# First batch's odd value tiles copied on GpSimd, block sums stored by one DMA each, and all instruction lists replaced

## The chip, the cores and the metric

The kernel runs on one core of one Trainium2 chip. The metric is the device time of one execution in microseconds (us). Before the change three runs took 917.28, 917.82 and 918.20 us (median 917.82). The profile comes from one further execution of 918.29 us; the span of its trace, from the first to the last profiled instruction, is 916.5 us, so 1.79 us lie around it.

## The reference

Windowed causal attention over 8 batches, 8 heads, 576 positions and 64 channels, followed by an RMS norm and a gated feed-forward layer over all 4608 tokens (512 channels, 1536 hidden):

```python
scores = (1 / sqrt(64)) * q @ k.T                    # per batch and head, 576 x 576
mask = (rel >= 0) & (rel < 64)                       # each position sees itself and the 63 before it
attn = softmax(where(mask, scores, -1e9))
x = (attn @ v).transpose(0, 2, 1, 3).reshape(4608, 512)
xn = x / sqrt(mean(x * x, -1) + 1e-6) * rms_g
g, val = xn @ w_gate, xn @ w_val                     # 512 -> 1536
out = (g * sigmoid(g) * val) @ w_out                 # 1536 -> 512
```

## The kernel before, in words

**Attention.** Heads go in pairs, n = 4 * batch + pair, since two heads of 64 channels fill 128 partitions. Tiles `q`, `kv` come by DMA; `kv` holds the keys (576 columns), the "even" value blocks (640 columns) and the "odd" ones (512 columns), which are the same values shifted by half a block of 64 rows, so that a window of two neighbouring blocks can always be read as one tile of 128 partitions. In `load_kv`, `odd_values()` loads them from DRAM a second time, by two DMAs of 64 partitions for each pair. TensorE (PE) makes the scores (`sc`), VectorE (DVE) masks them and finds the row's extreme (the custom operation into `p` or `pm`), ScalarE (ACT) takes the exponential and its row sum into `st`, DVE inverts the sum, and a scaling follows: for batches 0 and 1 on GpSimd (POOL), from then on on ACT. The weights are turned by TensorE (`tr`, copied out to `pt`) in batches 0 and 1. From batch 2 on, 32 x 32 blocks are moved between partitions (`moved`: 13 or 16 copies for a pair, dealt to POOL and ACT by the string `MOVE_ON`) and then turned by DVE. Products with the values (`xp`) follow, are copied to `xb`, squared and summed (`ssq`), the total goes through TensorE (`tot`), a chain of small DVE steps makes the inverse root, `rb` spreads it, and `xn` holds the normalised tokens as two float16 parts.

**Feed-forward.** There are nine tiles of 512 tokens. The weights come as float32 by DMA (`st`), are widened, scaled and split in two float16 parts (`wt`). Tiles 0 and 1 are plain products: `pg` and `pv` (gate and value), `th` (gated result), `h`, `po` (output), each by three float16 products. From tile 2 (`FIRST7`) on, the input side takes 7 block products in place of 8 (`bk`), from tile 3 the output side too. These need sums of weight blocks. `prepare(c, step)` makes them for the six columns c of the input weights while tile 1 runs: DVE adds blocks into `sum0`, `sum1` and `blk`; its inner `out` lets ACT round a sum to float16 (`hl`, first half), DVE subtract for the second half, and SP store both halves by two DMAs to the DRAM tile `sevens`. Three of the seven blocks need no sum; they are copied there from `wt` by 12 DMAs for each column (72 in all). `load_sevens` loads the blocks into a ring of 15 places in `wt`, refilled as TensorE is done with them. `prepare_out` does the same for the output weights (`wsum`, `whl`, `outs`) while tile 2 runs.

**Order.** Each engine runs its instructions in the order in which they stand, SP its DMA issues too. All calls are first recorded under names (engine letter and tile, `t` TensorE, `v` DVE, `s` ACT, `g` POOL, `y` SP), and `emit_recorded` writes them out in the order of five literal lists, `ORDER` and `ORDER_0` to `ORDER_3`. The waits follow from the data and from the buffers: `t2k`, for instance, is a pool of 8 tiles of 2 KB per partition that `th`, `hl`, `blk`, `whl`, `ot`, `p` and others share, and a tile that a DMA stores is free once the DMA has landed. `keep_warm` records up to 24 times 40 idle products (`warm`, 256 columns of ones, read by nobody); the lists take as many of them as they name, 26 before. Every recorded instruction carries the line of the helper that emits it, 589 before and 591 after; tiles tell them apart.

Of the kernel before, what the change touches and what calls it, by code (L numbers as in the profile page):

```python
# [27 lines left out]
P = 128  # L28
# [3 lines left out]
NKT = 5  # L32
# [30 lines left out]
MOVE_ON = "ga"  # L63
# [32 lines left out]
g.blocked y.q_3 y.kv_0*3 y.kv_1 t.sc_0_0*7 y.st_0_0 t.sc_0_0 v.gmx v.shifted v.ebias t.sc_0_0 v.one t.sc_0_0 v.pick  # L96
t.sc_0_1 v.ebias v.shifted t.warm_0 v.p_0_0_0 t.warm_0 y.kv_1 t.warm_0 v.p_0_0_0 s.p_0_0_0 v.p_0_0_0 y.st_1_0 v.p_0_0_1
t.sc_0_1*2 v.p_0_0_1 s.p_0_0_0 t.sc_0_1*2 v.p_0_0_0 y.kv_3 t.sc_1_0 s.p_0_0_1 t.sc_0_1*3 y.kv_2 t.warm_0*2 v.p_0_1_1
s.p_0_0_1 t.warm_0 y.kv_2 v.p_0_1_1 v.p_0_1_0 s.p_0_0_0 t.sc_1_0 y.kv_2 t.sc_1_0 v.p_0_1_0 t.sc_1_0*5 s.p_0_1_1
t.sc_1_0 y.q_4 t.sc_1_0 v.st_0_0 t.gps v.st_0_0 v.first_of v.p_1_0_0 s.p_0_1_0 v.floor y.st_0_1 v.first_of g.p_0_0_1  # L100
v.p_1_0_0 v.gmx y.kv_3 s.p_0_1_0 v.p_1_0_0 g.p_0_0_0 v.p_1_0_0 t.tr_0_0_1*2 y.kv_3 s.p_0_1_1 t.sc_1_1*2 v.pt_0_0_1
t.sc_1_1*3 g.p_0_0_0 t.sc_1_1*2 s.p_1_0_0 t.sc_1_1 v.st_0_1 v.p_1_0_1 t.tr_0_0_0*2 v.st_0_1 s.p_1_0_0 v.p_1_0_1
t.tr_0_0_0 g.p_0_1_0 v.p_1_1_1 t.sc_2_0 v.p_1_1_1 s.p_1_0_0 v.pt_0_0_0 t.sc_2_0 g.p_0_1_1 s.p_1_0_1 v.pt_0_0_0
v.p_1_1_0 t.tr_0_1_0 v.p_1_1_0 s.p_1_0_1 t.tr_0_1_0 t.tr_0_1_1 v.gmx t.tr_0_1_1 t.sc_2_0 s.p_1_1_0 t.xp_0_0 t.sc_2_0*2
v.st_1_0 t.sc_2_0 v.unit t.sc_2_0*4 v.st_1_0 t.xp_0_0 v.unit s.p_1_1_1 t.xp_0_0*2 v.p_2_0_0 g.p_1_0_1 t.xp_0_0*3
v.p_2_0_0 t.xp_0_0 s.p_1_1_1 t.sc_2_1 v.p_2_0_0*2 g.p_1_0_0 v.pt_0_1_0 t.sc_2_1 v.first_of t.sc_2_1*2 s.p_1_1_0
t.sc_2_1*2 v.p_2_0_1 t.xp_0_0*2 t.sc_2_1 g.p_1_0_0 s.p_2_0_0 t.sc_2_1 v.pt_0_1_1 t.tr_1_0_0 v.p_2_0_1 t.xp_0_1
# [419 lines left out]
def tile_window_attention_moe(  # L527
# [456 lines left out]
    def weigh(part, low, total):  # L984
        nc.scalar.activation(part, part, AF.Exp, bias=low, scale=-1.0, accum_out=total)
# [1207 lines left out]
```

## Time and profile before

| | |
|---|---|
| median of three runs | 917.82 us |
| profiled execution / span of its trace | 918.29 us / 916.5 us |
| TensorE busy | 898.9 us (98%) |
| VectorE busy | 715.9 us (78%) |
| ScalarE busy | 672.3 us (73%) |
| GpSimd busy | 376.5 us (41%) |
| DMA, mean over the span | 212 GB/s |

"Busy" of PE covers the modelled ends of pipelined products, so a stretch with PE busy throughout may still hold fewer products than another. The columns of a window row are the stretch, its length, then busy time and number of instructions of PE, weight loads, DVE, ACT and POOL, the granted clock of TensorE as a share of full, the busy share of the 16 DMA engines, and GB/s.

### The profile page before, as it was taken

The page shows a single profiled execution, that of the slowest core. Times are in us where ns is not written, and L with a number is a line of the kernel's source. Part 1 is how long each engine was busy: PE and PEld are TensorE (multiplying, and loading weights), DVE is VectorE, ACT ScalarE, POOL GpSimd, SP SyncE. Part 2 cuts the span into 40 slices and gives each one's busy share as a digit, 9 for nine tenths or more (in the row PEclk, how much of TensorE's full clock was granted, in tenths as well). Part 3 has the DMA queues.
Part 4 walks back from the last instruction along what each step waited for, and adds up shares of the span by engine and source line. Part 5 has one row for each costly group of instructions (what it writes and reads, how often), then busy time and mean ns, then how long its engine had stood idle before and what let it go on. Part 6 is the DMA issues. An engine that isn't in the chain of part 4 may idle for free.

```text
span 916.5 us, 24146 instructions
## 1 busy us (share of the span) xinstructions
PE 898.9 (98%) x8861; PEld 688.2 (75%) x8872; DVE 715.9 (78%) x2026; ACT 672.3 (73%) x1777; POOL 376.5 (41%) x506
## 2 busy tenths in 40 slices
PE   7899999999999999999999999999999999999998
PEld 4655554444448884688888888888888888888887
DVE  5898879799988888689879877888788767724760
ACT  5888988497877798699869986998697435614550
POOL 3456445354353464155524543454345222311230
PEclk9999999999999999999999999999999999999999
DMA  9695666676326985497877886777766767777623
GB/s 298 212 281 169 236 201 159 188 216 207 116 82 203 316 276 156 133 370 235 278 226 229 234 280 220 233 233 248 225 186 188 238 193 202 202 242 207 176 72 112
DMA packets 130854, 194.26 MB, mean 212 GB/s; under 512 B 30896, under 2 KB 60592, under 8 KB 130736
## 3 DMA queue, kind: packets, MB, share of 16 engines
q1 hardware_dynamic: 130160, 191.84, 68.4%
q8 instruction: 69, 1.13, 0.5%
q10 hardware_dynamic: 576, 0.88, 0.3%
q14 instruction: 49, 0.40, 0.1%
HBM read 166.73 MB, written 25.95 MB: 210 GB/s over the span
## 4 chain that ended last, share of the span: by engine, by line
PE 86%; DVE 7%; ACT 4%; DMA 2%; issue 1%; SPq 0%; ACTq 0%; POOL 0%; DVEq 0%
PE bk L589 59%; PE pv L589 6%; PE pg L589 6%; PE xp L589 4%; PE sc L589 4%; PE po L589 3%; ACT pm L589 2%; DVE th L589 1%; DVE wt L589 1%; DVE pm L589 1%; PE tr L589 1%; PE pw L589 1%; DVE ssq L589 1%; DVE sum L589 1%; DMA q<-q 1%
## 5 line engine op out<-in xcount | busy, mean ns | idle before, releaser
L589 PEld LDWEIGHTS <-wt 128*128 128x128 f16 x4128 | 402.4, 98 | 112.8 <-issue 8.1
L589 PE MATMUL bk<-xn,wt 128*128 128x256 f16 x2016 | 242.5, 273 | 1.8 <-DVE th L589 1.7
L589 PE MATMUL bk<-wt,wt 128*128 128x256 f16 x1440 | 176.9, 273 | 0.0
L589 POOL TENSOR_TENSOR hw<-th,hw 128x256 f16<-128x256 f32 x72 | 66.0, 934 | 254.1 <-ACT hw L589 194.2
L589 PE MATMUL bk<-hw 128*128 128x256 f16 x1512 | 169.4, 273 | 0.6 <-ACT ot L589 0.6
L589 PEld LDWEIGHTS <-hw 128*128 128x128 f16 x1512 | 146.7, 98 | 18.7 <-issue 1.8
L589 ACT ACTIVATE pm<-pm,st 128x128 f32<-128x128 f32 (+1 forms) x432 | 151.4, 388 | 8.3 <-DVE st L589 7.8
L589 POOL COPY pm<-pm 32x288 f32<-32x288 f32 (+1 forms) x169 | 84.0, 497 | 77.1 <-ACT pm L589 70.7
L589 ACT ACTIVATE th<-bk,hsc 128x256 f32<-128x256 f32 x126 | 59.3, 472 | 33.2 <-DVE bk L589 17.5
L589 DVE SCALAR_TENSOR_TENSOR th<-th,bk 128x256 f32<-128x256 f32 x126 | 52.5, 417 | 32.4 <-ACT th L589 31.9
L589 PE MATMUL pg<-xn,wt 128*128 128x512 f16 x288 | 74.5, 379 | 2.0 <-DVE th L589 1.8
L589 PE MATMUL pv<-xn,wt 128*128 128x512 f16 x288 | 73.0, 379 | 0.9 <-DVE th L589 0.7
L589 PEld LDWEIGHTS <-h 128*128 128x128 f16 x408 | 39.0, 98 | 45.8 <-issue 0.7
L589 ACT COPY pm<-pm 32x288 f32<-32x288 f32 (+1 forms) x146 | 60.7, 416 | 2.5
L589 POOL TENSOR_TENSOR h<-th,h 128x512 f16<-128x512 f32 x30 | 37.4, 1250 | 55.0 <-ACT h L589 51.8
L589 PE MATMUL po<-wt,h 128*128 128x512 f16 x264 | 59.0, 379 | 0.0
L589 POOL TENSOR_TENSOR xn<-xb,xn 128x448 f16<-128x448 f32 (+7 forms) x47 | 41.5, 898 | 35.8 <-ACT xn L589 33.4
L589 PE MATMUL sc<-kv,q 64*64 64x128 f32 (+1 forms) x1056 | 49.5, 280 | 6.3 <-DMA q<-q 6.0
L589 DVE TENSOR_TENSOR bk<-bk,s 128x512 f32<-128x512 f32 x42 | 29.2, 696 | 33.8 <-ACT pm L589 17.5
L589 DVE SCALAR_TENSOR_TENSOR th<-bk,th 128x256 f32<-128x256 f32 x126 | 52.2, 418 | 2.2
L589 PEld LDWEIGHTS sc<-kv,q 64*64 64x64 f32 x1056 | 37.2, 137 | 12.2 <-issue 10.1
L589 DVE CUSTOM_DVE_ANT_0 pm<-sc,blocked 128x128 f32<-128x128 f32 x192 | 44.3, 279 | 0.8 <-PE sc L589 0.8
(185 smaller groups left out, 1519.7 us busy)
## 6 DMA issues: line engine op xcount, KB each, us to landing
wt<-sevens SPq DMA_DIRECT2D x294, 256.0 KB, 3.4
hw<-outs SPq DMA_DIRECT2D x84, 384.0 KB, 5.3
kv<-kv SPq DMA_DIRECT2D x28, 608.0 KB, 4.6
q<-q SPq DMA_DIRECT2D x29, 288.0 KB, 5.1
kv<-kv SPq DMA_DIRECT2D x65, 128.0 KB, 5.9
st<-w_gate SPq DMA_DIRECT2D x6, 1024.0 KB, 7.4
st<-w_val SPq DMA_DIRECT2D x6, 1024.0 KB, 6.2
st_o<-w_out SPq DMA_DIRECT2D x6, 1024.0 KB, 5.1
```

Of the source, the lines that this page charges most:

```text
L589: steps[next(tensor) if name == "t" else name].popleft()()
```

## The change

What it does: the odd values of the four pairs of batch 0 (`ODD_BY`) are copied by POOL from the even ones in the same tile, in place of eight DMAs. `hl` holds its halves in the order in which DRAM wants them, so that one DMA stores both. `MOVE_ON` gives POOL two of three moves, not one of two. `SUMS` is empty, so the new path in `scores` is not taken. All five lists are replaced; they name 55 idle products.

```diff
-MOVE_ON = "ga"
+MOVE_ON = "gga"
+SUMS = ()
+ODD_BY = {0: 'g', 1: 'g', 2: 'g', 3: 'g'}
 ORDER = """
-y.kv_0 s.q_2 s.q_0 y.kv_0 y.gsb s.q_1 g.mask s.q_0 y.kv_1 g.mask*2 y.kv_1 g.mask y.kv_2 g.mask*2 y.kv_3 g.mask
+y.kv_0 s.q_0 y.kv_1 s.q_1 g.mask v.unit y.kv_0 s.q_0 v.one g.mask t.warm_0 s.q_2 y.gsb g.mask t.warm_0 g.mask t.warm_0
...
         def odd_values():
+            if n in ODD_BY:
+                copy = copy_on(ODD_BY[n])
+                copy(odd[0:D], even[0:D, : NKT - 1, :])
+                copy(odd[D:P], even[D:P, 1:, :])
+                return
             src = kv[n, :, S : S + NKT * P].rearrange("p (u c) -> p u c", c=P)
             nc.sync.dma_start(out=odd[0:D], in_=src[0:D, : NKT - 1, :])
             nc.sync.dma_start(out=odd[D:P], in_=src[D:P, 1:, :])
...
         def out(src, o):
-            src = src.rearrange("p w k f -> p (w k f)")
-            hl = wk.tile([P, 2, TT], F16, tag="t2k", name=f"hl_{c}_{step}", bufs=T2K)
+            src = src.rearrange("p w k f -> p w (k f)")
+            hl = wk.tile([P, 2, 2, TT // 2], F16, tag="t2k", name=f"hl_{c}_{step}", bufs=T2K)
 
             def rest():
-                nc.vector.tensor_tensor(hl[:, 1], src, hl[:, 0], ALU.subtract)
-                for j in range(2):
-                    nc.sync.dma_start(
-                        out=sevens[c][:, o, :, j].rearrange("p w k f -> p w (k f)"),
-                        in_=hl[:, j].rearrange("p (w n) -> p w n", w=2),
-                    )
+                nc.vector.tensor_tensor(hl[:, :, 1], src, hl[:, :, 0], ALU.subtract)
+                nc.sync.dma_start(out=sevens[c][:, o].rearrange("p w a k f -> p (w a k f)"), in_=hl.rearrange("p w a n -> p (w a n)"))
 
-            unfinished.append([partial(nc.scalar.copy, hl[:, 0], src), rest])
+            unfinished.append([partial(nc.scalar.copy, hl[:, :, 0], src), rest])
```

Instructions that change in number, counted over the whole program: 29 more idle products and their weight loads; on POOL 8 copies of 64 x 512 (`kv`) and 49 moves more; on ACT 49 moves fewer; on SP 8 loads fewer and 24 stores of `hl` in place of 48. DVE has the same number.

Three places where the lists move instructions. First ACT's queue at the program's start, where ACT issues the loads of the queries (`q_135` is pair 0, `q_137` pair 1, `q_139` pair 2; pair 0 comes in two pieces). Before:

```order
L589 DMA q_139<-q 128x576
L589 DMA q_135<-q 128x320
L589 DMA q_137<-q 128x576
L589 DMA q_135<-q 128x256
L589 ACT_TABLE_LOAD
```

After:

```order
L591 DMA q_135<-q 128x320
L591 DMA q_137<-q 128x576
L591 DMA q_135<-q 128x256
L591 DMA q_139<-q 128x576
L591 ACT_TABLE_LOAD
```

Pair 0's first piece moves from second to first, its second piece from fourth to third. On PE, ten idle products now stand behind the first one and ahead of the first `sc`, where before `sc` was the first product.

Second SP's queue while tile 1 of the feed-forward runs, around the stores of the first column's sums (`hl_0_2`, `hl_0_4`, `hl_0_5`; `sevens0` to `sevens5` are the six columns in DRAM, `q_12` a load of queries). Before, after 57 of the 72 copies from `wt`:

```order
L589 DMA sevens4_132<-wt8_95 128x2x128 x2
L589 DMA sevens4_132<-wt9_96 128x2x128
L589 DMA sevens0_128<-hl_0_2_2173 128x2x256
L589 DMA sevens4_132<-wt9_96 128x2x128 x2
L589 DMA sevens0_128<-hl_0_2_2173 128x2x256
L589 DMA sevens4_132<-wt9_96 128x2x128 x3
L589 DMA sevens5_133<-wt10_97 128x2x128 x2
L589 DMA sevens5_133<-wt11_98 128x2x128 x4
L589 DMA sevens0_128<-hl_0_4_2183 128x2x256
```

After, where 50 copies stand ahead of the first store:

```order
L591 DMA sevens4_132<-wt8_95 128x2x128 x2
L591 DMA sevens0_128<-wt1_88 128x2x128
L591 DMA sevens0_128<-hl_0_2_2202 128x1024
L591 DMA sevens0_128<-hl_0_4_2212 128x1024
L591 DMA q_12_2253<-q 128x576
L591 DMA sevens4_132<-wt8_95 128x2x128 x3
L591 DMA sevens0_128<-hl_0_5_2214 128x1024
```

The last store of the first column (`hl_0_7`) stood behind all 72 copies before, and stands behind 60 now; column 1's first store stands behind all 72 in both.

Third POOL in batch 0, where it scales the weights (`p`, with the inverse sums `st`; `kv_138` and `kv_140` are the tiles of pairs 1 and 2). Before, the scalings of pair 1 and the start of pair 2:

```order
L589 TENSOR_TENSOR p_0_0_187<-p_0_0_187,st_0_189 128x64
L589 TENSOR_TENSOR p_1_0_199<-p_1_0_199,st_1_201 128x256
L589 TENSOR_TENSOR p_1_1_200<-p_1_1_200,st_1_201 128x256
L589 TENSOR_TENSOR p_0_0_209<-p_0_0_209,st_0_211 128x256
L589 TENSOR_TENSOR ssq_196<-xb_195 128x576
```

After:

```order
L591 TENSOR_TENSOR p_0_0_187<-p_0_0_187,st_0_189 128x64
L591 TENSOR_TENSOR p_1_0_199<-p_1_0_199,st_1_201 128x256
L591 COPY kv_138<-kv_138 64x512 x2
L591 TENSOR_TENSOR p_1_1_200<-p_1_1_200,st_1_201 128x256
L591 TENSOR_TENSOR p_0_0_209<-p_0_0_209,st_0_211 128x256
L591 TENSOR_TENSOR p_0_0_209<-p_0_0_209,st_0_211 128x64
L591 TENSOR_TENSOR p_0_1_210<-p_0_1_210,st_0_211 128x256
L591 TENSOR_TENSOR ssq_196<-xb_195 128x576
```

Two copies stand between the two scalings of a pair; pairs 0, 2 and 3 have theirs likewise.

## Rows read from the trace of the kernel before

**Rows 1.** Page, part 4: chain that ended last, by engine.

```profile
PE 86%; DVE 7%; ACT 4%; DMA 2%; issue 1%; SPq 0%; ACTq 0%; POOL 0%; DVEq 0%
```

**Rows 2.** Windows: stretch, length, busy (instructions) per engine, clock, DMA share, GB/s.

```profile
0.00:5.30 5.30, 0.00 (x0) 0.02 (x1) 0.00 (x0) 1.28 (x1) 2.57 (x14) 1.00 0.62 198
5.30:14.00 8.70, 7.88 (x84) 5.06 (x84) 5.07 (x49) 5.16 (x25) 1.47 (x4) 1.00 1.04 327
14.00:24.00 10.00, 9.69 (x123) 6.65 (x124) 7.52 (x51) 7.12 (x26) 5.24 (x9) 1.00 1.06 322
24.00:31.70 7.70, 7.42 (x88) 5.02 (x85) 7.52 (x39) 6.39 (x22) 4.85 (x8) 1.00 1.01 312
31.70:44.00 12.30, 10.04 (x171) 7.19 (x171) 10.88 (x41) 10.81 (x30) 3.98 (x6) 1.00 0.46 168
...
180.00:196.00 16.00, 13.50 (x105) 6.58 (x100) 13.55 (x43) 15.18 (x49) 5.48 (x12) 1.00 0.83 249
196.00:300.00 104.00, 104.00 (x898) 59.29 (x897) 92.79 (x241) 82.10 (x232) 49.12 (x61) 1.00 0.52 159
300.00:332.00 32.00, 30.35 (x326) 26.73 (x325) 26.37 (x82) 26.57 (x76) 17.07 (x19) 1.00 0.97 304
332.00:910.00 578.00, 577.83 (x6093) 500.16 (x6092) 432.68 (x1167) 406.83 (x1084) 216.63 (x275) 1.00 0.70 216
```

**Rows 3.** Chain of waits in order of time, 0 to 60 us: start, length, what.

```profile
2.15 5.06 DMA q<-q
...
8.75 1.06 PE sc L589 x16
10.57 1.28 PE sc L589 x15
...
37.51 0.69 PE sc L589 x18
```

**Rows 4.** Timeline, start, and PE at 9 and 30 us: start, duration, instruction, count.

```profile
0.75 1.85 ACTq L589 DMA_DIRECT2D q<-q  x4
...
9.75 0.82 PE L589 MATMUL warm<-one 128*128 128x256 bf16 x3
...
30.77 1.05 PE L589 MATMUL warm<-one 128*128 128x256 bf16 x8
```

**Rows 5.** Waits until 48 us: total, times, longest.

```profile
DVE p L589 <- PE sc L589: 5.0, 5, 1.8
```

**Rows 6.** Page, part 6: loads of odd values; count, KB each, us to landing.

```profile
kv<-kv SPq DMA_DIRECT2D x65, 128.0 KB, 5.9
```

**Rows 7.** Groups of POOL until 44 us: shapes and count, busy, mean ns, idle before.

```profile
L589 POOL TENSOR_TENSOR p<-p,st 128x256 f32<-128x256 f32 x16 | 9.6, 613 | 17.9 <-DVE first_of L589 7.8 <-DVE st L589 7.1 <-ACT p L589 2.2
...
L589 POOL CAST blocked<-mask 128x192 bf16<-128x192 f32 x1 | 0.3, 342 | 0.1
```

**Rows 8.** Page, part 5: the moves on POOL and on ACT.

```profile
L589 POOL COPY pm<-pm 32x288 f32<-32x288 f32 (+1 forms) x169 | 84.0, 497 | 77.1 <-ACT pm L589 70.7
...
L589 ACT COPY pm<-pm 32x288 f32<-32x288 f32 (+1 forms) x146 | 60.7, 416 | 2.5
```

**Rows 9.** Timeline of SP, 150 to 198 us: start, length, DMA issues.

```profile
149.54 16.23 SPq L589 DMA_DIRECT2D sevens<-wt  x29
165.87 0.41 SPq L589 DMA_DIRECT2D sevens<-hl  x1
```

**Rows 10.** Timelines of ACT and DVE, 172 to 198 us; idle before in brackets.

```profile
178.14 0.62 ACT L589 CAST hl<-sum 128x512 f16<-128x512 f32 x1 [5.00 <-DMA sevens<-hl]
```

**Rows 11.** Chain of waits, 160 to 200 us.

```profile
175.71 2.33 DMA sevens<-hl
...
194.68 2.75 PE pv L589 x12
```

**Rows 12.** Chain of waits, 284 to 335 us.

```profile
302.18 4.87 DMA outs<-whl
```

**Rows 13.** Instructions of tile hl: count, duration min/median/max in ns, first and last start.

```profile
L589 DVE TENSOR_TENSOR hl<-sum,hl x24: 631/684/1232, 156.4 to 266.0; 128x512 f16<-128x512 f32 x24
```

More of the change, by code (lines that the diff above doesn't have):

```diff
@@ L199 @@
+v.ssq_1 t*2 s.pm_8 t g.below v.ssq_1 t g.below*4 v.ssq_1 t g.three_of s.pm_8 v.ssq_1 g.three_of t g.three_of g.below*2
+v.ssq_1 t g.below s.pm_8 g.below g.three_of*2 v.ssq_1 t v.ssq_1 t s.pm_8 v.ssq_1 t*2 v.ssq_1 t v.st_8 v.ssq_1 t v.st_8
+t v.ssq_1 s.pm_8 t v.ssq_1 t s.pm_8 v.ssq_1 t s.pm_8 t s.pm_8 t*2 s.pm_8 t s.pm_8 t s.pm_8*4 g.pm_8 s.pm_8 g.pm_8*3
 """
 ORDER_1 = """
[L201 to L202 removed]
@@ new lines @@
+y.wt1 t*5 v.th_2_3_0 t*2 s.xb_3 g.pm_9 t*2 y.wt2 t*3 s.xb_3 t*2 v.pm_9 t g.wsum_3_1 y.wt0 t*4 s.kv_14 t y.wt3 t v.pm_10
+t v.pm_10 t y.wt4 s.pm_10 t v.pm_10 t*2 g.ssq_3 v.pm_10 t s.s1 t v.pm_9 t*4 s.h_2_3 t*2 v.pm_10 t*2 v.u2 g.h_2_2 t
+s.pm_10 t*4 s.pm_10 v.pm_10 t*2 v.pm_10 t*2 v.pm_10 s.th_2_3_1 t g.h_2_3 t v.pm_9 t*2 v.bk2 s.pm_10 t*5 s.pm_10
+v.th_2_3_1 t*4 s.th_2_4_0 t v.whl_2_5 t*3 s.wt7 t*2 v.pm_10 t*2 v.th_2_4_0 t*3 v.th_2_3_1 s.th_2_3_1 t y.wt0 t*3
+s.pm_10 y.outs t v.th_2_3_1 t*3 s.pm_10 t y.outs v.th_2_3_1 t*3 v.wsum_3_0 t s.u2 t y.outs t*2 v.wsum_3_1 t s.h_2_3 t
@@ new lines @@
+y.wt3 t*3 s.th_5_2_0 v.sb_5_1 y.kv_28 t*3 v.pm_11 s.wt7 t y.kv_28 t v.sa_5_1 t*2 s.pm_9 t*2 v.sa_5_1 y.wt0 t*3
+v.th_5_2_0 s.th_5_1_1 t y.wt2 t*2 s.hw t v.th_5_2_0 t*3 v.th_5_1_1 t*2 s.u2 t*2 v.th_5_1_1 t*4 s.hw v.sb_5_1 t*3
+v.st_27 t*2 v.st_27 t v.bk5 t g.hw s.pm_9 t*3 s.pm_9 t*2 v.hw s.hw t*3 s.pm_9 t*2 g.hw t y.wt5 s.pm_9 t*2 s.th_5_2_0 t
+y.hw t*3 s.pm_9 t y.kv_27 v.th_5_2_0 t*2 s.pm_9 t*2 s.pm_9 v.th_5_2_0 t y.wt1 t*2 s.pm_9 v.u2 t*2 y.wt1 t s.pm_9 t*2
+s.s1 y.wt4 t v.sb_5_2 t g.pm_9 t*2 y.kv_27 t s.th_5_2_1 t*3 g.pm_9 s.hw t y.wt3 t v.th_5_2_1 t*2 g.pm_9 t y.wt4 v.bk2
@@ new lines @@
+s.u2 t*35 v.ot_7_3 t*7 y. t*4 y. t*5 y. t*4 y.hw t*17 y.hw v.ot_7_4 t*7 y. t*4 y. t*4 y. t*21 v.ot_7_5 t*7 y. t*4 y.
+t*4 y. t*5 y.hw t*16 y.hw s.ot_7_6 t*7 y. t*4 y. t s.s1 t*3 y.wt6 t*4 y. t*5 y.wt6 s.wt7 t*12 y.wt7 v.bk2 t*7
+s.th_8_0_0 t*5 y.wt0 s.u2 v.th_8_0_0 t*4 v.th_8_0_0 t*4 s.hw t*4 y.wt0 v.bk5 t g.hw t*6 s.th_8_0_0 t*4 v.th_8_0_0 t
+y.wt1 s.s1 t*4 v.th_8_0_0 t*4 v.sb_8_0 t*3 v.u2 t y.wt1 t*7 s.th_8_0_1 t*4 v.th_8_0_1 t y.wt2 t*3 v.bk2 t*5 v.th_8_0_1
+t*2 s.th_8_1_0 t*2 y.wt2 v.sa_8_0 t s.wt7 t*2 v.th_8_1_0 t*3 v.sa_8_0 t*3 v.th_8_1_0 t*2 s.hw t y.wt3 t*3 s.th_8_0_1 t
@@ L984, in weigh @@
     def weigh(part, low, total):
-        nc.scalar.activation(part, part, AF.Exp, bias=low, scale=-1.0, accum_out=total)
+        more = {} if total is None else {"accum_out": total}
+        nc.scalar.activation(part, part, AF.Exp, bias=low, scale=-1.0, **more)
     def products_of_pair(n, qk, first, ahead):
```

829 lines of the change are left out of this document (409 added, 420 removed).

## The prediction

> **What bounds the kernel now.** I read the chain by engine first [rows 1]: 86% of it is PE. The windows then tell where PE is not the limit [rows 2]. From 332 to 910 us PE is busy 577.83 of 578.00 us: no list can shorten that stretch, only lengthen it. What can be won lies in three places. Until 5.3 us PE does nothing, and until 44 us it waits again and again: of the 38.7 us from 5.3 to 44.0 the four windows show 35.03 busy, and "busy" there counts slow products. From 180 to 196 us PE stands 16.00 - 13.50 = 2.5 us, from 300 to 332 us 32.00 - 30.35 = 1.65 us. From 196 to 300 us it is busy throughout.
>
> In the start DVE is nearly full: 5.07 + 7.52 + 7.52 + 10.88 = 30.99 us of 38.7, so 7.7 us idle, of which 5.0 us are waits for scores from PE [rows 2, 5]. The DMA engines are full from 5.3 to 31.7 us (shares 1.04, 1.06, 1.01) [rows 2].
>
> **The change, part by part.** The sum is made against the profiled execution, 918.29 us (span 916.5 and 1.79 around it); it is 0.47 us above the median of the runs shown.
>
> *A, the start (to 44 us).* Pair 0's two pieces of queries move up one place each on ACT's queue. Four issues take 1.85 us there [rows 4], 0.46 each. The fourth is what the chain hangs on: issued at 2.15 us, landed 5.06 us later [rows 3]. So the scores come about 0.5 us earlier.
>
> The idle products come early, and that bears on the rate of PE. The granted clock in the rows reads 1.00 from the first window on, but the products don't run at one rate: three idle products take 0.82 us at 9.75 us, eight take 1.05 us at 30.77 us [rows 4], and scores take 2.34 us for 31 at 8.75 and 10.57 us against 0.69 us for 18 at 37.51 us [rows 3], that is 75 and 38 ns. The slow ones look like the level of 1.2 GHz, the later ones like 2.4 GHz; before the slow ones PE had done nothing until 5.3 us. With ten idle products ahead of the first score the rate may rise before the scores come: 31 x 0.037 = 1.1 us. The Trainium skill (TensorE: Matmul & The Clock Gate, "What's actually happening") says that the throttled state is the default and that activity releases it; by that rule the granted clock's column is wrong here and the whole 1.1 us is to be had, and by the column nothing is. I take the durations' side.
>
> The 29 additional idle products cost 29 x 1.05 / 8 = 3.8 us if all of them stood on the path. Ten stand in the first 5.3 us, which are empty; the other 19 (2.5 us) stand where PE waits for DVE. I take nothing for them, with 2.5 us as the upper end. If that cover is gone, each costs 0.13 us.
>
> Eight loads of 128 KB go [rows 6], 1.05 MB or 3.3 us at 322 GB/s [rows 2], from a stretch in which the DMA engines are full, and weights and keys land earlier by up to that. What ends on it doesn't show as one wait, so I take 0.9 us; the ends are 0 and 3.3.
>
> The copies on POOL aren't in the trace. A cast of 192 columns takes 342 ns [rows 7], a move of mostly 288 columns 497 ns [rows 8]; 1.6 ns more for each column gives 0.86 us for 512. Eight are 6.9 us; bounds are 2.7 (at 342 ns each) and 9.8 (two scalings of 256 columns, 613 ns each, for one copy) [rows 7]. POOL sat idle 17.9 us before its scalings [rows 7], so the work fits. But two copies now stand between the two scalings of a pair, and the second scaling, then its `tr`, comes up to 1.7 us later. Only the last pair's delay can reach the end of the start, since the earlier pairs' values are asked for later. I take nothing, upper end 1.7.
>
> DVE's list has almost the same work ahead of the first `rb` (127 recorded steps before, 130 now), so A can't give more than DVE's idle time, and realistically not more than its waits for scores: 5.0. Taken: 0.5 + 1.1 + 0.9 = **-2.5 us**, from -5.0 to +2.0.
>
> *B, the block sums.* The chain passes through a store's landing at 175.71 us and from there through ACT and DVE to PE's late product at 194.68 us [rows 11]. ACT stood 5.00 us until a store of `hl` had landed [rows 10]: `hl` could not have a `t2k` buffer, because earlier halves waited in SP's queue. The first pair of halves was ready at 156.4 + 0.7 = 157.1 us [rows 13], but SP issued 29 copies from `wt` one after another from 149.54 us, 0.56 us each, and came to the first store at 165.87 us [rows 9]. The last store of column 0 stood behind 72 copies, 7 stores and 10 other issues, and now behind 60, 3 and 6: 20 issues or 11 us less, more than the 5.00 us. Late next is column 1's first store, behind 91 issues in both lists; before, nothing stood for it. I take **-2.2 us** of the 2.5, from -2.5 to 0.
>
> *C, output weights' sums (300 to 332 us).* Here the chain passes through a store of `whl` that takes 4.87 us to land [rows 12], with DMA shares of 0.97 [rows 2]. Nothing in the kernel's code changes there, only the list. Half of 1.65 us: **-0.8 us**, from -1.65 to +1.65.
>
> *D, the moves.* 49 go from ACT (416 ns) to POOL (497 ns) [rows 8]: ACT -20.4 us, POOL +24.4 us, most of it where PE is full and POOL idle for 361 of 578 us [rows 2]. The turn that follows on DVE is due long after them. **0**, from 0 to +1.5.
>
> *E, what the new lists open elsewhere.* They may delay a product anywhere between 44 and 332 us, where DVE is 82 to 89% busy in the windows shown [rows 2]. **+0.5 us**, from 0 to +4, the sum of today's B and C.
>
> Sum: -2.5 - 2.2 - 0.8 + 0 + 0.5 = -5.0, so 913.3 us for the profiled execution and 912.8 beside the median; I say **913.0 us**.
>
> **Rivals.**
>
> *The start gives nothing (0.17).* DVE had 31 us of work and keeps them; if its waits for scores are only replaced by waits for POOL, loads or the root's chain, A is 0 and the time is 918.29 - 2.5 = 915.8, or 915.4 beside the median. For it speaks DVE's fullness from 24 to 31.7 us (7.52 of 7.70) [rows 2]; against it that the 5.0 us of waits are before that.
>
> *Slower: SP's queue stands still elsewhere (0.14).* The new list puts reloads of the ring (`wt1<-sevens0`) between the stores of later columns, and `wt1` ahead of `wt0`. A reload has to wait until TensorE is done with the place, and what stands behind it in the queue waits too. If that is a store of `hl` or `whl`, `t2k` runs out and ACT stands as it does today for 5.00 us [rows 10]. It decides from about 5 us of standstill in front of a store, twice: B gives 0, C +1.65, and a second place like today's B 2.5, with A at -1.0: 918.29 + 3.15 = 921.4.
>
> *The copies stand on the path (0.09).* Then A is +1.7 in place of -2.5 and the time 917.5. Against it stands POOL's idle time [rows 7].
>
> *DVE is slowed by POOL's reads (0.07).* Subtractions of `hl`, all of one shape, took from 631 to 1232 ns [rows 13]; something stretches them. The Trainium skill (SBUF — State Buffer, "Who interferes with whom") says that a DVE instruction with two inputs in SBUF contends with a GpSimd instruction that reads SBUF; the spread agrees, though it shows no cause. The lists put 20 of the 49 moves on POOL before 332 us, 10 us at 497 ns [rows 8]; each can hold DVE for its own length at most and only where the two meet, so I set a tenth to a third of it, 1 to 3 us, in the stretch where B and C are won. At 3 the gain of B and C is gone: 918.29 - 2.5 + 0.5 = 916.3.
>
> **How the numbers follow.** The forecast (A and B come, 909 to 915) has 0.53. About 0.2% or 1.8 us is what a measurement of this kernel can tell from no change, so faster is below 916.0, slower above 919.7. Faster: 0.53, most of the first rival (0.12) and some of the last (0.03): 0.68. Slower: 0.14 and what the copies could cost beyond their price (0.03): 0.17. Same: 0.15. Low end: A -5.0, B -2.5, C -1.65 give 909.1. High end: between the rivals of no gain (917.5) and the slower one (921.4); 918.8 leaves about 0.12 above and 0.08 below. So 909.0 to 918.8; the forecast's own range is 909 to 915.
>
> **What would show it.** A: the first `sc` before 5.0 us, sixteen scores in about 0.7 us from then on, the first `rb` about 2.5 us earlier, DVE's waits for scores under 3 us. B: no wait of ACT for a store of `hl`, PE busy over 15.5 of 16 us around 190 us. C: under 1 us of PE's idle time near 305 us. D: PE full from 330 us on. I am wrong if `rb` comes no earlier, if SP stands in front of a store after 180 us, or if PE waits for DVE in a place where it does not now.

## The result

The changed kernel takes 910.45 us (median of 5 runs, 909.83 to 910.81), the kernel before, run beside it, 918.10 us (5 runs, 917.28 to 918.63). The ratio is 0.9916, with a 95% interval from 0.9902 to 0.9929: 7.6 us or 0.84% faster. 913.0 us had been forecast, with 909.0 to 918.8 as the range. The profiled execution took 910.21 us, its span is 908.4 us; against the one of before (918.29 us, span 916.5 us) 8.1 us are gone.

Five marks that both programs have show where. The first `rb` comes at 40.31 us (43.26 before), the first product of tile 0's output, `po`, at 134.74 us (138.14), the first `po` of tile 1 at 239.75 us (246.01), the first `bk` of tile 2 at 274.02 us (280.41), the first product of tile 3's output sums, `bk<-hw`, at 432.40 us (440.00). So the start gives 2.95 us, or 3.40 if what follows from it until tile 0's output is counted with it; the stretch of the block sums gives 2.86 us, the way to tile 2 0.13 us, the stretch of the output weights' sums 1.21 us, and what comes after it 0.49 us. Together that is 8.09 us.

### The profile page after: what moved, and what is told of

The parts are those of the page before. It is cut to its first block, busy times and chain, and to the rows that moved or that the text cites. A ratio compares the mean times of both kernels' runs of the same rounds, so it can differ in the third digit from the quotient of the medians.

```text
span 908.4 us, 23998 instructions
## 1 busy us (share of the span) xinstructions
PE 897.0 (99%) x8901; PEld 688.5 (76%) x8901; DVE 711.8 (78%) x2026; ACT 652.3 (72%) x1728; POOL 396.8 (44%) x563
## 4 chain that ended last, share of the span: by engine, by line
PE 95%; DVE 1%; DMA 1%; ACT 1%; SPq 0%; POOL 0%; issue 0%; POOLq 0%; ACTq 0%; DVEq 0%
PE bk L591 64%; PE pv L591 7%; PE po L591 7%; PE pg L591 7%; PE xp L591 4%; PE sc L591 3%; PE pw L591 1%; PE tr L591 1%; PE pw_o L591 1%; DMA wt<-sevens 1%; DMA kv<-kv 1%; DVE p L591 0%; SPq L591 0%; ACT p L591 0%; PE warm L591 0%; PE rb L591 0%
## 5 line engine op out<-in xcount | busy, mean ns | idle before, releaser
L591 POOL COPY pm<-pm 32x288 f32<-32x288 f32 (+1 forms) x218 | 104.1, 477 | 93.9 <-ACT pm L591 85.3
L591 PE MATMUL pg<-xn,wt 128*128 128x512 f16 x288 | 69.5, 379 | 0.1
L591 PE MATMUL pv<-xn,wt 128*128 128x512 f16 x288 | 69.4, 379 | 0.0
L591 POOL TENSOR_TENSOR xn<-xb,xn 128x448 f16<-128x448 f32 (+7 forms) x47 | 38.9, 838 | 52.2 <-ACT xn L591 50.8
L591 DVE TENSOR_TENSOR bk<-bk,s 128x512 f32<-128x512 f32 x42 | 29.2, 696 | 28.0 <-PE bk L591 22.4
L591 PE MATMUL sc<-kv,q 64*64 64x128 f32 (+1 forms) x1056 | 45.9, 274 | 1.6 <-DVE st L591 1.6
L591 ACT CAST xn<-xb 128x64 f16<-128x64 f32 (+7 forms) x63 | 25.7, 426 | 28.6 <-DVE xb L591 28.0
L591 POOL TENSOR_TENSOR hw<-sb,hw 128x512 f16<-128x512 f32 x36 | 41.8, 1161 | 2.2 <-PE bk L591 1.2
```

Source lines behind the costliest of these rows:

```text
L591: steps[next(tensor) if name == "t" else name].popleft()()
```

## The profile after

The chain that ended last, by engine (page, part 4; compare [rows 1]):

```profile
PE 95%; DVE 1%; DMA 1%; ACT 1%; SPq 0%; POOL 0%; issue 0%; POOLq 0%; ACTq 0%; DVEq 0%
```

PE's share rises from 86 to 95%: almost nothing but products is left on the path. The windows, cut as in [rows 2] (the last one ends at 900 us, since the program ends 8 us earlier):

```profile
0.00:5.30 5.30, 3.64 (x33) 2.61 (x33) 0.25 (x2) 1.28 (x1) 2.57 (x14) 1.00 0.65 219
5.30:14.00 8.70, 7.94 (x116) 5.95 (x116) 7.11 (x61) 7.42 (x37) 4.01 (x8) 1.00 1.02 367
14.00:24.00 10.00, 9.45 (x118) 6.51 (x119) 8.56 (x47) 8.33 (x26) 7.06 (x13) 1.00 0.91 342
24.00:31.70 7.70, 6.78 (x93) 4.54 (x89) 7.63 (x31) 6.67 (x22) 6.11 (x11) 1.00 0.66 204
31.70:44.00 12.30, 9.41 (x166) 6.49 (x165) 11.49 (x42) 8.59 (x21) 6.53 (x7) 1.00 0.25 96
...
180.00:196.00 16.00, 16.00 (x136) 8.16 (x134) 12.61 (x33) 12.76 (x38) 7.84 (x15) 1.00 0.60 207
196.00:300.00 104.00, 104.00 (x866) 61.33 (x866) 91.33 (x254) 77.11 (x224) 48.85 (x65) 1.00 0.53 171
300.00:332.00 32.00, 31.41 (x338) 27.75 (x337) 26.55 (x74) 28.22 (x82) 19.68 (x27) 1.00 0.91 285
332.00:900.00 568.00, 568.00 (x6006) 491.53 (x6004) 422.99 (x1148) 383.67 (x1024) 219.66 (x297) 1.00 0.68 217
```

PE does 116 instructions from 5.3 to 14 us where it did 84, in the same busy time: its products are shorter. DVE has 7.11 us of work there instead of 5.07. In 180 to 196 us PE no longer stands (16.00 of 16.00 us, 13.50 before), in 300 to 332 us it stands 0.59 us instead of 1.65. The timeline of PE at the start (start, duration, instruction, count, idle before):

```profile
1.66 2.53 PE L591 MATMUL warm<-one 128*128 128x256 bf16 x11 [1.66 <-DVE one L591]
4.12 1.13 PE L591 MATMUL sc<-kv,q 64*64 64x128 f32 x20
5.18 1.29 PE L591 MATMUL warm<-one 128*128 128x256 bf16 x10
...
8.25 0.66 PE L591 MATMUL sc<-kv,q 64*64 64x128 f32 x16 [0.71 <-DVE st L591]
```

Eleven idle products take 2.53 us (230 ns each), the ten behind the first twenty scores 1.29 us (129 ns); sixteen scores take 0.66 us (41 ns), where [rows 3] had 1.06 us for sixteen. The windows' clock column reads 1.00 throughout, as before, and yet the durations show a slow stretch at the start. The clock records in the traces settle this: the changed kernel's trace has none before 4.90 us and that of the kernel before none before 11.86 us, the first record in each is at full speed, and the column counts a stretch without a record as 1.00. The durations change where the first record starts (the scores of the changed kernel from 4.96 us on); I call that the rise of the rate. DVE's waits for scores until 44 us (total, times, longest), and all that PE waits for between 44 and 905 us:

```profile
DVE p L591 <- PE sc L591: 5.0, 3, 3.8
```

```profile
PE bk L591 <- ACT ot L591: 0.6, 1, 0.6
PE bk L591 <- DMA wt<-sevens: 0.6, 1, 0.6
```

3.8 of the 5.0 us are now the wait for the first score of all (in the kernel before, DVE's idle time until 5.4 us is put down to the load of `gsb`); the other two make 1.2 us. The wait for a reload of the ring is new (it ends at 320.2 us). SP comes to the first store of `hl` at 156.85 us instead of 165.87 us [rows 9], 2 us after the first pair is ready (154.9 us), and the second pair goes with it:

```profile
156.85 0.90 SPq L591 DMA_DIRECT2D sevens<-hl  x2
```

The copies of the odd values take 608 ns (median), a move on POOL still about as long as before; 49 of these went there from ACT:

```profile
L591 POOL COPY kv<-kv x8: 601/608/615, 11.5 to 26.2; 64x512 f32<-64x512 f32 x8
```

```profile
L591 POOL COPY pm<-pm 32x288 f32<-32x288 f32 (+1 forms) x218 | 104.1, 477 | 93.9 <-ACT pm L591 85.3
```

## The experiments

All were timed against the kernel before, which took 918.17, 918.16 and 917.84 us in the three sets of runs. The table gives the median of each (4 to 12 runs), the ratio's interval, and from its one profiled execution the first `sc`, the first `rb`, and the length of three stretches: from `rb` to the first `po` of tile 1 (block sums), from the first `bk` of tile 2 to the first `bk<-hw` of tile 3 (output weights' sums), and from there to the end of the span. The stretch from `po` to `bk` takes 34.3 to 34.4 us in all. Differences from the changed kernel are between medians of different sets, and each ratio's interval is 2.2 to 3.2 us wide; but every run of experiments 1, 3, 4 and 8 and of the changed kernel with the old start is slower than every run of the changed kernel (911.22 us at least, against 910.81 at most).

| kernel | us | ratio | sc | rb | rb to po | bk to hw | hw to end |
|---|---|---|---|---|---|---|---|
| before | 918.1 | | 5.31 | 43.26 | 202.75 | 159.59 | 476.51 |
| after | 910.45 | 0.9902 to 0.9929 | 4.12 | 40.31 | 199.44 | 158.38 | 476.02 |
| after, no idle products ahead of the scores | 912.61 | 0.9927 to 0.9951 | 3.96 | 43.49 | 199.64 | 158.16 | 476.01 |
| after, none in the gaps | 912.43 | 0.9918 to 0.9951 | 4.11 | 42.02 | 199.47 | 159.81 | 476.01 |
| after, queries in the old order | 913.65 | 0.9944 to 0.9968 | 5.74 | 43.39 | 199.71 | 158.32 | 476.17 |
| before, with idle products ahead | 918.03 | 0.9990 to 1.0014 | 5.45 | 42.80 | 202.02 | 161.06 | 476.56 |
| after, odd values loaded late | 933.46 | 1.0153 to 1.0180 | 4.12 | 64.40 | 199.47 | 157.68 | 476.01 |
| after, odd values loaded with the even | 910.31 | 0.9894 to 0.9926 | 4.11 | 40.23 | 199.46 | 157.69 | 476.02 |
| before, with the new start | 914.53 | 0.9948 to 0.9974 | 4.12 | 41.70 | 201.21 | 158.15 | 476.59 |
| after, with the old start | 913.18 | 0.9927 to 0.9955 | 5.43 | 43.47 | 199.90 | 157.94 | 476.02 |
| after, two stores | 911.08 | 0.9907 to 0.9942 | 4.12 | 40.38 | 200.46 | 157.61 | 476.34 |
| before, one store | 915.95 | 0.9962 to 0.9986 | 5.35 | 43.27 | 201.27 | 158.15 | 476.43 |
| after, 48 moves back on ACT | 911.90 | 0.9915 to 0.9946 | 4.12 | 40.35 | 199.44 | 158.38 | 477.23 |
| after, ones first, a load later | 910.94 | 0.9901 to 0.9936 | 4.88 | 40.83 | 199.44 | 158.41 | 476.06 |

**1. No idle products ahead of the first score.** The eleven `t.warm_0` ahead of the first `t.sc_0_0` go from `ORDER`:

```diff
-... v.one g.mask t.warm_0 s.q_2 y.gsb g.mask t.warm_0 g.mask t.warm_0
+... v.one g.mask s.q_2 y.gsb g.mask*2
 ...
```

> The changed kernel without the eleven idle products ahead of the first score; all else as it is. Theory (the idle products raise the rate of PE before the scores come): the scores until about 10 us take some 75 ns each again instead of some 41, the rate rises later, the first rb comes 1 to 2 us later, and the time goes from 910.4 to about 911.5 (911.2 to 912.5). Rival (the granted clock's column is right and the idle products do nothing): scores keep about 41 ns at 8 us, the first score is at 4.1 us as before, time 910.4, plus or minus 0.3.

The timeline of PE:

```profile
3.96 1.33 PE L590 MATMUL sc<-kv,q 64*64 64x128 f32 x20 [3.96 <-DMA q<-q]
5.23 2.32 PE L590 MATMUL warm<-one 128*128 128x256 bf16 x10
7.48 1.53 PE L590 MATMUL sc<-kv,q 64*64 64x128 f32 x18
```

The first score comes 0.16 us earlier, but the ten idle products behind the first scores take 2.32 us instead of 1.29, and the next eighteen scores 85 ns each. The trace's first clock record comes at 13.16 us, not at 4.90. `rb` comes 3.2 us later. The idle products ahead raise the rate: shown. The profiled run is the slowest of five (911.34 to 913.95), so 3.2 us is an upper end; by the medians it is 2.2 us. In this run the rate also falls later on, and here the clock's column shows it; it can have cost little, 0.3 us, since the twenty scores ahead of `tot` start 2.9 us late already (36.19 us, 33.29 in the changed kernel):

```profile
40.40:43.90 3.50, 3.44 (x31) 2.09 (x21) 3.23 (x14) 3.50 (x11) 0.56 (x1) 0.51 0.03 7
```

**2. Idle products ahead, in the kernel before.** `v.one` and 17 `t.warm_0` go to the head of `ORDER`, nothing else:

```diff
-y.kv_0 s.q_2 s.q_0 y.kv_0 ...
+v.one t.warm_0*17 y.kv_0 s.q_2 s.q_0 y.kv_0 ...
 ...
```

> The kernel before with one thing added: the vector of ones is written first on DVE and seventeen idle products stand ahead of the first score; they end before the loads land. Theory (idle products raise the rate of PE): the scores from 5.3 us on take about 40 ns instead of 75, the first rb comes up to 1.1 us earlier than 43.3 us, time about 917.0 instead of 918.1 (916.8 to 917.8). Rival (the rate is as the column says, 1.00 from the start, and the idle products do nothing): scores stay at 75 ns until 10 us, 918.1, plus or minus 0.3. Second rival (the rate rises but DVE's list sets the end): scores at 40 ns, rb within 0.3 us of 43.3, time 917.8 to 918.2.

Two windows, the stretch in which PE waits for data and the one behind it:

```profile
5.30:8.00 2.70, 1.32 (x24) 1.06 (x25) 1.69 (x18) 1.33 (x7) 0.00 (x0) 1.00 1.05 348
8.00:11.00 3.00, 3.00 (x39) 1.95 (x37) 1.22 (x11) 1.88 (x11) 0.17 (x1) 0.52 0.98 332
```

The first twenty scores take 0.77 us (38 ns), then PE is busy for 1.32 of 2.70 us, and the granted clock falls to 0.52. `rb` comes 0.46 us earlier and the time doesn't change. All three theories missed a part: the rate rises, and is lost again.

**3. No idle products in the gaps.** The reverse of the first: the eleven stay, the 26 `t.warm_0` behind the first score go (the list of before had six of this name, so this takes away more than the change had added).

```diff
-t.sc_0_0*3 y.kv_2 t.warm_0 v.p_0_0_0 t.warm_0 v.p_0_0_1 y.kv_3 t.warm_0 ...
+t.sc_0_0*3 y.kv_2 v.p_0_0_0 v.p_0_0_1 y.kv_3 ...
```

> The changed kernel without the 26 idle products of its first group that stand between the scores and turns of the first pairs; the eleven ahead of the first score stay. Theory (the rate of PE, once up, is kept only while PE does not stand; with the gaps empty it is lost again as in the run of the kernel before with idle products ahead alone, whose granted clock fell to 0.52 in 8 to 11 us): a stretch at a granted clock well under 1 before 15 us, scores of 70 ns or more there, the first rb 2 to 3.2 us later, time 912.5 to 913.5. Rival (the rate, once up, stays up, and the products in the gaps are filling): the first rb within 0.4 us of 40.3, time 910.0 to 910.8.

```profile
4.11 1.33 PE L588 MATMUL sc<-kv,q 64*64 64x128 f32 x20
5.61 0.66 PE L588 MATMUL sc<-kv,q 64*64 64x128 f32 x2 [0.16 <-DMA q<-q]
6.77 1.44 PE L588 MATMUL sc<-kv,q 64*64 64x128 f32 x16 [0.51 <-DVE st L588]
8.91 1.34 PE L588 MATMUL sc<-kv,q 64*64 64x128 f32 x20 [0.70 <-DVE st L588]
```

The scores stay at 67 to 90 ns until 10 us: the rate did not rise at all there (first clock record at 14.42 us), rather than rise and fall, as I had expected. `rb` comes 1.7 us later, the time is 2.0 us up. The products in the gaps are not filling; without them those ahead are worth little.

**4. The queries' old order.** Only ACT's four loads change places:

```diff
-s.q_0 ... s.q_1 ... s.q_0 ... s.q_2
+s.q_2 ... s.q_0 ... s.q_1 ... s.q_0
```

> The changed kernel with the four loads of queries on ACT in the order of before (pair 2 first). Theory (the first score hangs on the second piece of pair 0's queries, one place later on ACT's queue): first score at about 4.6 instead of 4.1 us, first rb up to 0.5 us later, time about 910.9. Rival (something else, DVE's list or the rate of PE, sets the end of the start): first score later, rb within 0.15 us of 40.3, time 910.4, plus or minus 0.3.

```profile
1.66 2.53 PE L591 MATMUL warm<-one 128*128 128x256 bf16 x11 [1.66 <-DVE one L591]
5.74 1.33 PE L591 MATMUL sc<-kv,q 64*64 64x128 f32 x20 [1.55 <-DMA q<-q]
7.01 2.32 PE L591 MATMUL warm<-one 128*128 128x256 bf16 x10
```

The first score comes 1.62 us later, not 0.5. The chains of waits of this run and of the first experiment show why: the load that it hangs on starts later and then also takes longer, here 4.42 us with another load of queries issued ahead of it, there 3.17 us. That the other load is what slows it was not tested.

```profile
1.19 4.42 DMA q<-q
```

```profile
0.75 3.17 DMA q<-q
```

PE stands 1.55 us behind the eleven idle products, and the rate that they would have brought isn't there for the next ten (2.32 us). So this one line costs 3.2 us by the medians, as much as the whole old start (2.7) or more: its gain and that of the idle products are not two terms that add, each needs the other.

**5. The odd values loaded.** Once at the places where the copies stood in the list, once directly behind the values (in the list two `y.kv_n` in place of two `g.kv_n`, or behind the `y.kv_n` of the values).

```diff
-ODD_BY = {0: 'g', 1: 'g', 2: 'g', 3: 'g'}
+ODD_BY = {}
```

> The changed kernel with the odd values of the first batch loaded again by two transfers of 128 KB each, at the places in the list where the copies' sources were loaded and copied. Theory (the freed 1.05 MB is worth 0.9 us in a stretch where the DMA engines are full): the values and weights land later, the first rb comes 0.5 to 3.3 us later, time about 911.3 (910.7 to 913.5). Rival (the transfers were hidden, nothing is gained by the copies): 910.4, plus or minus 0.3. Second rival (the copies on POOL hold up the scalings): up to 0.5 us faster, 909.9.

> The changed kernel with the odd values loaded again, but each pair's two transfers directly behind the transfer of its values on SP, ahead of the weights, and no copies on POOL. Theory (the freed 1.05 MB, or 3.3 us of the DMA engines, was worth about 0.9 us): the weights' loads land later and the first rb comes 0.5 to 3.3 us later, time 911.0 to 913.5. Rival (the transfers were hidden; the 23 us of the kernel with the loads at the copies' place came from their place in the queue alone): 910.4, plus or minus 0.4.

At the copies' place SP issues the loads behind three weight loads of 1 MB, four of them from 12.98 us on, and PE stands for two of them (SP's timeline; PE's waits until 60 us):

```profile
12.98 5.97 SPq L591 DMA_DIRECT2D kv<-kv  x4
```

```profile
PE xp L591 <- DMA kv<-kv: 17.2, 2, 12.2
```

That run tells of the place in the queue, not of the transfers; it is 20 us more than any theory allowed. The two waits are 17.2 of the 24.1 us by which `rb` is late. While PE stands, the granted clock falls to its lower level (1.2 GHz) and stays there until 39.3 us, which is part of the rest; how much was not separated:

```profile
15.40:39.30 23.90, 13.55 (x103) 8.94 (x103) 6.59 (x34) 5.63 (x17) 3.73 (x6) 0.50 0.45 149
```

The second one tells of the transfers: 910.31 us, `rb` at 40.23 us. The windows of that kernel:

```profile
14.00:24.00 10.00, 9.53 (x118) 6.57 (x118) 8.52 (x47) 8.35 (x26) 5.76 (x11) 1.00 1.05 323
24.00:31.70 7.70, 6.78 (x93) 4.54 (x89) 7.63 (x31) 6.67 (x22) 3.74 (x7) 1.00 1.04 378
```

The DMA engines are full here, where they are at 0.91 and 0.66 in the changed kernel, and PE and DVE do the same work in the same time. Neither the freed transfers nor the copies change anything that can be told.

**6. The start exchanged.** The kernel before with the first list of the changed one and the branch of `odd_values` that copies, and the reverse (the edit is that of the first):

```diff
 WARM = 40, 24
+ODD_BY = {0: 'g', 1: 'g', 2: 'g', 3: 'g'}
-ORDER = (list of before)
+ORDER = (list of after)
 ...
```

> The kernel before with the first list of the changed kernel and its copies of the odd values on POOL; the later lists and the two stores as before. Theory (the start is worth 3.4 us, and nothing that follows takes it back): the first rb at about 40.3 us, all later marks 3.0 to 3.4 us earlier than before, time about 914.8 (914.4 to 915.2). Rival (the later lists were made for the old start, so part of it is lost again): time 915.5 to 918.

> The changed kernel with the first list of before and the odd values loaded; the later lists and the merged store stay. Theory (the terms add: block sums 2.9, output weights' sums 1.2, later 0.5): time 910.4 + 3.4 = 913.8 (913.4 to 914.3), first rb at 43.3 us. Rival (with the late start the transfers of the sums come late again and ACT stands once more): time 914.5 to 918.

The old start costs the changed kernel 2.7 us; the stretches behind it keep their lengths within 0.5 us, so the terms add, as expected (913.8 forecast, 913.18 measured). The new start gives the kernel before 3.6 us, 914.53 against 914.8 expected, but not as expected: `rb` is only 1.6 us earlier in the profiled run, and the stretches of the sums are 1.5 and 1.4 us shorter although their lists are the old ones. PE's timeline shows why `rb` gains less:

```profile
4.12 1.33 PE L590 MATMUL sc<-kv,q 64*64 64x128 f32 x20
5.38 2.32 PE L590 MATMUL warm<-one 128*128 128x256 bf16 x10
7.63 0.87 PE L590 MATMUL sc<-kv,q 64*64 64x128 f32 x18
```

The instructions and their starts are those of the changed kernel until 4.12 us, and yet the rate rose only at about 7.6 us (first clock record at 7.58) instead of 4.9. That makes 1.0 us of the 1.4 by which `rb` is later than in the changed kernel; the rest comes where the granted clock falls to half once more, ahead of `rb`:

```profile
38.30:40.40 2.10, 2.10 (x47) 1.52 (x34) 1.89 (x8) 2.10 (x10) 0.00 (x0) 0.50 0.03 8
```

The early rise is thus not assured by the list, and the twelve runs of this kernel spread from 913.14 to 918.72 us. What decides it was not settled.

**7. One store or two.** The new order with two stores, and the old order with one (the edit is that of the first; the layout of `hl` goes back with it, and the list gets a second store behind each).

```diff
 ...
-                nc.sync.dma_start(out=sevens[c][:, o].rearrange("p w a k f -> p (w a k f)"), in_=hl.rearrange("p w a n -> p (w a n)"))
+                for j in range(2):
+                    nc.sync.dma_start(
+                        out=sevens[c][:, o, :, j].rearrange("p w k f -> p w (k f)"),
+                        in_=hl[:, j].rearrange("p (w n) -> p w n", w=2),
+                    )
 ...
```

> The changed kernel with the halves of each block sum stored by two transfers again, one right behind the other at the place of the merged one; the order of all else is the new one. Theory (most of the gain between 44 and 246 us is that fewer issues stand ahead of the stores on SP: 20 fewer at 0.56 us were named, of them 3 or 4 by the merge and 12 by the order): ACT waits for no store or for well under 1 us, the second tile's results keep their place, time 910.4 to 911.0. Rival (the merge itself carries the gain): ACT stands some 2 to 5 us for a store of hl, PE loses 1 to 2.5 us between 180 and 196 us, time 911.5 to 913.

> The kernel before with the halves of each block sum stored by one transfer (at the place of the second of the two), all lists else as they were. Theory (the order of SP's queue carries the gain, the merge little): the first store still leaves SP at about 166 us, ACT still stands about 4 to 5 us, time 917.5 to 918.2. Rival (the merge carries it): ACT's wait falls under 2 us, PE stands under 1 us between 180 and 196 us, time 915.8 to 917.

The new order with two stores keeps 2.3 of the 3.3 us between `rb` and `po`; ACT waits 1.2 us for a store, PE stands 0.86 us (window of 180 to 196 us):

```profile
180.00:196.00 16.00, 15.14 (x104) 7.22 (x105) 14.33 (x41) 13.95 (x42) 9.14 (x15) 1.00 0.68 199
```

By the medians the second store costs 0.6 us, inside both intervals. In the old order the kernel with one store is 2.2 us faster by the medians, though SP still comes to it at 166.76 us and ACT still stands 4.1 us; that is more than my theory gave it:

```profile
166.76 0.41 SPq L586 DMA_DIRECT2D sevens<-hl  x1
```

```profile
ACT hl L586 <- DMA sevens<-hl: 4.1, 2, 3.8
```

```profile
180.00:196.00 16.00, 14.94 (x111) 7.18 (x108) 14.89 (x45) 15.62 (x50) 6.57 (x13) 1.00 0.68 216
```

So ACT's wait was the wrong gauge: it shrank by 0.9 us, PE's idle time by 1.44 us. But not all of that is shown to be the merge's. In the same window PE stands 2.50 us in the kernel before, 1.81 and 1.42 us in the two other kernels with its later lists and two stores (experiment 2 and the first of experiment 6), and in the last of these ACT waits for no store of `hl` at all. One store in the old order leaves 1.06 us, two in the new order 0.86, one in the new order none. So the merge is worth 0.4 to 1.4 us there in the old order and 0.9 in the new one, the order 0.6 to 1.6 us with two stores and 1.1 with one; only both together leave PE nothing to wait for. Of the gain of the old order with one store another 1.4 us lie, in the profiled runs, in the stretch of the output weights' sums, whose length differs from run to run with the same list (C below).

**8. Moves back on ACT.** The second and the eighth move of a pair on ACT, at the same places: 170 on POOL, 145 on ACT, within one as before the change.

```diff
-            move(m, p, copy_on(MOVE_ON[i % len(MOVE_ON)]), k, qq)
+            move(m, p, act_copy if i in (1, 7) else copy_on(MOVE_ON[i % len(MOVE_ON)]), k, qq)
```

> The changed kernel with two more moves of each pair on ACT, at the places in the program where POOL did them, so that ACT and POOL do about as many as before. Theory (the 0.5 us that are won after 440 us come from ACT's relief): PE waits for th on DVE again for some tenths of a us between 440 and 660 us, the stretch from the first bk of the third tile to the end takes 476.4 to 476.6 instead of 476.02 us, time about 910.8. Rival (they come from the searched list alone): that stretch takes 476.0 to 476.1 us, time 910.4, plus or minus 0.2.

All marks until 432.4 us are the same to 0.05 us, and then 1.2 us are lost, more than either theory said (1.5 us by the medians). 1.1 of them lie between 432 and 464 us and between 557 and 619 us. The windows of this kernel there, and of the changed one:

```profile
432.00:464.30 32.30, 32.15 (x384) 28.11 (x377) 27.00 (x91) 22.35 (x71) 13.19 (x19) 1.00 0.67 228
...
557.80:619.20 61.40, 61.30 (x704) 53.98 (x705) 48.42 (x144) 57.27 (x165) 29.07 (x39) 1.00 0.74 242
```

```profile
432.00:464.30 32.30, 32.30 (x388) 28.47 (x381) 27.27 (x93) 21.48 (x68) 13.82 (x20) 1.00 0.68 233
...
557.80:619.20 61.40, 61.40 (x714) 54.51 (x712) 50.39 (x142) 56.13 (x159) 31.91 (x46) 1.00 0.76 248
```

ACT has 1 us more in each, POOL less, and PE 4 and 10 products fewer, in breaks too short for the list of waits. That this list needs the moves off ACT is shown, the single wait isn't. What the moves are worth by themselves isn't shown either: the kernel before, with as many on ACT and its own list, takes 476.51 us from `hw` to the end, and this one 477.23.

**9. A trial to better it.** `v.one` at the head of the list, seven more idle products ahead, and one load of values behind five reloads near 311 us.

```diff
-WARM = 40, 24
+WARM = 48, 24
-y.kv_0 s.q_0 y.kv_1 ... v.unit y.kv_0 s.q_0 v.one ...
+v.one t.warm_0*7 y.kv_0 s.q_0 y.kv_1 ... v.unit y.kv_0 s.q_0 ...
-y.kv_16 ... y.outs ... y.wt4 ... y.wt5 ... y.wt1 ... y.wt2 ... y.wt0
+y.outs ... y.wt4 ... y.wt5 ... y.wt1 ... y.wt2 ... y.wt0 ... y.kv_16
```

> A trial to better the changed kernel: the vector of ones is written first on DVE, eighteen idle products instead of eleven stand ahead of the first score, and one load of values near 311 us goes behind five reloads of the ring on SP. Theory (PE's first work comes about a us earlier and the rate rises before the first score; the wait of 0.6 us for a reload near 320 us goes): the first twenty scores take about 0.8 instead of 1.13 us, the first rb at 39.9 to 40.2 us, time 909.4 to 910.0. Rival (the first score hangs on its loads at 4.1 us and the later chain on DVE): the start gives nothing, only the 0.6 us near 320 us are won or, given back later, none: 909.9 to 910.6.

```profile
0.93 4.02 PE L591 MATMUL warm<-one 128*128 128x256 bf16 x18 [0.93 <-DVE one L591]
4.88 0.87 PE L591 MATMUL sc<-kv,q 64*64 64x128 f32 x20
```

PE starts 0.73 us earlier, but the eighteen products run at the slow rate almost to their end, past the landing of the loads, and the first score is 0.76 us late; the trace's first clock record comes at 5.14 us, where the changed kernel has it at 4.90. The wait for a reload stays at 0.6 us. 910.94 us: no better. No version that beats the changed kernel beyond the interval was found.

## Why the prediction was right, and where not

The direction and the size were right; inside the start (A) one term was nothing and two were too small, and D was wrong. That the sum for A came so near is in part luck.

**A: -2.5 us forecast; -2.95 us at `rb`, -3.40 us at tile 0's output.** The queries' order was priced at one issue, 0.5 us; the load also lands sooner after its issue, and PE's work holds together: 3.2 us when undone. The rate of PE was priced at 1.1 us, by the durations and against the clock column. That was the right side (experiments 1 and 3, each about 2 us when undone), and the column had no record there to go by. By the Trainium skill (TensorE: Matmul & The Clock Gate, "What's actually happening"), the throttled state is the default and activity releases it; the trace agrees, 230 ns and then 129 ns for the same idle product. The freed transfers were priced at 0.9 us; they are worth nothing (experiment 5): until 44 us no wait of PE or DVE for a weight's load is listed in either kernel. The copies cost nothing, as forecast, and took 0.61 us each, not 0.86. The idle products cost nothing, as forecast, but the step saw the ones in the gaps as free filling; without them the rate does not rise before 14 us. (It also counted ten ahead of the scores and 19 elsewhere; the list has eleven, and 18 more than before elsewhere.) The sum came out near because the 0.9 us that weren't there stood for part of what the other two gave beyond their price.

**B: -2.2 us forecast, -2.86 us measured.** The step held: SP comes to the first store 9.0 us earlier (3.4 of them are the earlier start), no wait of ACT for a store is left, and PE is busy for all of 180 to 196 us (over 15.5 of 16 was named). Of the 2.86 us, 2.50 are PE's idle time, which went whole where the step had taken 2.2; the other 0.36 us lie in stretches in which PE counts as busy and were not tracked down. The mechanism is only a part of it, though: with the new start alone ACT's wait is gone and PE still stands 1.42 us (experiment 7).

**C: -0.8 us forecast, -1.21 us measured, but the new list is not shown to be its cause.** With the old lists that stretch took 159.59, 158.15, 158.15 and 161.06 us, with the new ones 157.61 to 159.81 us. The same list differs by up to 2.9 us; why was not settled. The changed kernel lies in the middle, 0.6 us of it in the wait that ends at 320.2 us.

**D: 0 forecast, from 0 to +1.5; -0.49 us measured after 432 us.** The step looked at POOL's idle time and not at what ACT gives up. ACT is busy for 56 of 61 us in such a stretch, and 48 moves more on it cost 1.2 us in the new list (experiment 8). The sign was wrong; how much of the 0.49 us is the moves and how much the list stays open.

**E: +0.5 us forecast.** One new wait of 0.6 us, inside C's stretch.

**The rivals.** That the start gives nothing: no, but each of three small edits, taken away alone, brings most of it back (2.0, 2.2 and 3.2 us of 2.7). That SP stands still at the reloads: it does, for 13.0 us in nine waits for `bk` between 180 and 332 us (4.5 us in four before), but ACT waits for no store, and PE waits for one reload, 0.6 us. That the copies stand on the path: no. That DVE is slowed by POOL's reads: DVE's subtraction for `hl` took 621 to 1160 ns, as spread as in [rows 13], with 29% more moves on POOL; and when 26 of the moves before 432 us go back to ACT (experiment 8), all marks until then stay the same to 0.05 us. So no.

**The signs.** DVE's waits for scores stayed at 5.0 us, where under 3 had been named; without the first score they are 1.2 us. Two signs of being wrong came by the letter: at the start PE now waits for DVE where it did not (`sc` for `st`, 1.6 us in two waits), and SP stands in front of stores after 180 us (22.4 us in seven waits until `hl` itself is ready, 11.6 us in ten before). Neither took the gain: `rb` is earlier and ACT waits for no store. They were drawn too sharp.

## What to carry to other kernels

Price an edit at the start of a program together with what it keeps running: an early load, idle products ahead of the first score and idle products in the gaps were worth 2 to 3 us each by removal, more together than the whole start; of the three only idle products ahead were tried alone, and gave nothing. Before relieving a full resource, ask whether the path's end waits for it; eight loads less from full DMA engines gave nothing. When a queue issues in order, its place decides: the same eight loads cost nothing behind their neighbours and 23 us behind the weights, of which 17.2 us were the waits themselves.

## What was not expected of the hardware

The same idle product took 230 ns and, 3 us later, 129 ns, while the granted clock's column read 1.00: the column is not to be trusted ahead of the trace's first clock record (4.90 us here, 14.42 us in experiment 3). The same instructions at the same times until 4.12 us brought the faster rate at 4.9 us in one profiled execution and at 7.6 us in another. And starting PE at 0.93 us instead of 1.66 did not bring it earlier: of eighteen products in 4.02 us nearly all were slow.

Where the rate rose late in the new start, it also fell once more ahead of `rb`: the column reads 0.50 to 0.52 somewhere between 38.3 and 43.9 us in experiments 1, 3 and 4 and in the first kernel of 6, and `rb` lost 0.2 to 0.4 us more there. The changed kernel's profiled run has no such fall. Over its five runs the mean granted clock is 1.0 in the two fastest (909.83 and 910.21 us) and 0.998 in the other three (910.45 to 910.81 us).
